# Down projection of the second token pair as seven block products, with gate and up operands stored once and read back

## The chip, the cores and the metric

The kernel runs on one core of one Trainium2 chip. The metric is the device time of one execution in microseconds (us); lower is better. The profile of a kernel is one further execution, recorded instruction by instruction on the chip. The engines of a core go by short names here: PE (TensorE, the matrix unit), DVE (VectorE), ACT (ScalarE), POOL (GpSimd), and SP, whose queue starts most of the transfers (DMA) between DRAM and on-chip memory (SBUF). PE writes into PSUM, from which DVE and ACT read.

## The reference, cut to what matters

```
x = A_x                                        # 2048 tokens, 576 features
g = sigmoid((x * gate_w).sum(-1, keepdims=True))
a = linear_attention(x, wqkv, wo)              # 32 heads
b = (gelu(x @ w_gate) * (x @ w_up)) @ w_down   # 576 -> 4608 -> 576
return g * a + (1 - g) * b
```

Everything is float32. Each factor is held as a sum of a high and a low part (float32r), and a product is three PE passes: high by high, high by low, low by high.

## The kernel before, in words

The attention part comes first, up to about 300 us. It leaves the gated attention output, 16 tiles of 128 tokens, in DRAM (`ga_d`), and the gate factors in `gate`. The rest of the span is the feed-forward part, and that is where the change lies.

**The loop.** Tokens are taken in two "pairs" of 1024, each pair as two halves of 512. The 4608 hidden features are taken in 18 blocks of 256 (`NF2`), each as two halves of 128. The loop at L830 runs `n` from 0 to 35 (`NQD` = 36): 18 blocks for the first pair, then the same 18 for the second. One turn has a gate half, `gu_steps(0)`, and an up half, `gu_steps(1)`. Each half has seven steps, s1, s6, s2, s7, s5, s4, s3, one for each of the seven block products of a Strassen-Winograd scheme over (two token halves) x (two feature halves). A product is seven matmuls of 128x512 into one PSUM bank (L664), with a stationary operand from `W[0]` (gate) or `W[1]` (up).

**Gate half.** s1's bank is copied to the tile `p1` by ACT (L715), and s2 then adds its product into the same bank, so s2 has to wait until that copy has read it. DVE forms sums of the other banks (L720, L735, L740, L749, L764), and ACT takes the gelu into four tiles `es[0]` to `es[3]`.

**Up half.** Here DVE multiplies `es[i]` by the up results (`up`, L701). In s5 and s3 the factor is first put into `p1`, the same tile as above; so the `p1` copy of the next gate half has to wait until the last `up` has read it. `high` (ACT, L704) and `low` (DVE, L707) split each `es[i]` into the tile `hs[i]`. In an ordinary turn the splits of s3's result are put off to the next gate half (`late`, L773).

**Down projection.** `down(n - 1, t)` (L780) runs one turn late, in between the steps: eight calls, one for each 128 tokens, each of 12 matmuls of 128x288 (two feature halves x three passes x two column halves) into a pair of PSUM banks, of which there are two pairs. One DVE instruction for each call (L794) multiplies by the gate factor and adds to the accumulator `acc[t]`, which was loaded with the attention output. In turn 18 four calls stand ahead of the gate half, and after the last turn eight calls end the kernel.

**Operands.** For every turn of both pairs, SP fetches the raw weights (`w_fetch`, L605), POOL forms four sums of blocks (`w_sums`, L608), ACT writes high parts and POOL low parts into `W[m]` (`w_split`, L614). `W[0]` and `W[1]` exist once each; `W[m]` can be rewritten only after PE has finished the half that reads it. `wd` is split by ACT and DVE (`d_prep`, L653). Between turns 2 and 13 POOL also forms sums of the second pair's tokens (`sums_ahead`, L669): on even turns SP fetches a piece (L674) and POOL adds. In turn 17 `renew` reloads the token operands for the second pair. Only the operands of turn 0 (`wp_d`) were made earlier, stored in DRAM and read back on the ACT queue (L627, L807).

**Order.** Everything is written out by hand: each engine executes its instructions in the order in which the code issues them, and waits on semaphores.

## Time and profile before

| What | us |
|---|---|
| Median of three timed runs | 1574.14 |
| Lowest and highest of them | 1573.69 and 1574.91 |
| The profiled execution | 1574.42 |
| Its span in the profile | 1572.7 |

| Engine | busy us | share of the span |
|---|---|---|
| PE matmul | 1556.8 | 99% |
| PE weight load | 1383.3 | 88% |
| DVE | 903.0 | 57% |
| POOL | 849.7 | 54% |
| ACT | 584.1 | 37% |

The span is the time from the first to the last recorded instruction; some 1.7 us of the profiled execution lie outside it. A row of a timeline gives start, duration, engine, source line, operation, output and inputs, and in brackets the idle time just before it and what ended it. PE's matmuls overlap at their ends, so the distance between two starts is what a group costs, and not its duration. The granted PE clock is at full speed throughout.

### The profile page before, as it was taken

The page shows a single profiled execution, that of the slowest core. Times are in us where ns is not written, and L with a number is a line of the kernel's source. Part 1 is how long each engine was busy: PE and PEld are TensorE (multiplying, and loading weights), DVE is VectorE, ACT ScalarE, POOL GpSimd, SP SyncE. Part 2 cuts the span into 40 slices and gives each one's busy share as a digit, 9 for nine tenths or more (in the row PEclk, how much of TensorE's full clock was granted, in tenths as well). Part 3 has the DMA queues.
Part 4 walks back from the last instruction along what each step waited for, and adds up shares of the span by engine and source line. Part 5 has one row for each costly group of instructions (what it writes and reads, how often), then busy time and mean ns, then how long its engine had stood idle before and what let it go on. Part 6 is the DMA issues. An engine that isn't in the chain of part 4 may idle for free.

```text
span 1572.7 us, 21574 instructions
## 1 busy us (share of the span) xinstructions
PE 1556.8 (99%) x8651; PEld 1383.3 (88%) x8651; DVE 903.0 (57%) x1265; ACT 584.1 (37%) x848; POOL 849.7 (54%) x677
## 2 busy tenths in 40 slices
PE   8999999999999999999999999999999999999998
PEld 8999788888888888888888888888888888888887
DVE  6443766465555555655555556565555555566555
ACT  6544555334333333343333323334333333333331
POOL 1400112366777777667765648655665566555650
PEclk9999999999999999999999999999999999999999
DMA  5611435712322222212211185111221121111201
GB/s 201 196 50 38 154 116 182 258 55 76 111 70 96 83 89 82 69 69 84 90 56 56 55 313 172 56 56 55 75 72 56 56 65 67 55 56 62 80 21 61
DMA packets 47964, 146.04 MB, mean 93 GB/s; under 512 B 3824, under 2 KB 20872, under 8 KB 45944
## 3 DMA queue, kind: packets, MB, share of 16 engines
q1 hardware_dynamic: 43544, 128.02, 23.9%
q10 hardware_dynamic: 2592, 9.31, 1.6%
q0 software_dynamic: 1728, 7.34, 1.2%
q8 instruction: 68, 1.11, 0.3%
q14 instruction: 32, 0.26, 0.1%
HBM read 121.16 MB, written 23.49 MB: 92 GB/s over the span
## 4 chain that ended last, share of the span: by engine, by line
PE 93%; DVE 3%; issue 1%; ACT 1%; DMA 1%; POOL 1%; SPq 0%; ACTq 0%; POOLq 0%; DVEq 0%
PE bank L664 50%; PE pair L788 29%; PE bank L169 7%; PE bank L333 3%; PE pair L524 2%; PE pair L220 1%; DMA xc<-xs 1%; POOL xo L476 1%; DVE e L701 1%; DVE h L707 0%; PE den L428 0%; PE pair L169 0%; DMA raw<-wkv 0%; PE pair L406 0%; DVE r L511 0%
## 5 line engine op out<-in xcount | busy, mean ns | idle before, releaser
L788 PEld LDWEIGHTS pair<-wd,h 128*128 128x128 f32 x3456 | 490.9, 189 | 26.4 <-DVE acc L794 3.1
L788 PE MATMUL pair<-wd,h 128*128 128x288 f32 x3456 | 505.1, 295 | 3.1 <-DVE acc L794 2.6
L664 PE MATMUL bank<-xo,wu 128*128 128x512 f32 x1764 | 434.2, 392 | 0.6 <-DVE p L740 0.5
L664 PE MATMUL bank<-xo,wg 128*128 128x512 f32 x1764 | 429.8, 392 | 1.2 <-ACT p L715 1.2
L794 DVE SCALAR_TENSOR_TENSOR acc<-pair,gate,acc 128x576 f32<-128x576 f32 x288 | 234.8, 816 | 267.9 <-PE pair L788 267.9
L664 PEld LDWEIGHTS bank<-xo,wg 128*128 128x128 f32 x1764 | 325.9, 188 | 66.7 <-ACT p L715 2.0
L664 PEld LDWEIGHTS bank<-xo,wu 128*128 128x128 f32 x1764 | 322.2, 188 | 60.9 <-DVE p L740 1.5
L704 ACT ACTIVATE h<-e 128x512 fp32r<-128x512 f32 x144 | 90.8, 630 | 403.5 <-DVE e L701 395.4
L618 POOL TENSOR_TENSOR wu<-wuraw,wu 128x768 fp32r<-128x768 f32 x35 | 70.0, 1999 | 277.4 <-ACT wu L617 277.4
L710 ACT ACTIVATE e<-e 128x512 f32<-128x512 f32 x108 | 68.3, 632 | 299.7 <-DVE e L740 118.0
L707 DVE TENSOR_TENSOR h<-e,h 128x512 fp32r<-128x512 f32 x144 | 124.8, 868 | 47.3 <-ACT h L704 47.1
L618 POOL TENSOR_TENSOR wg<-wgraw,wg 128x768 fp32r<-128x768 f32 x35 | 64.8, 1851 | 124.5 <-ACT wg L617 124.5
L169 PE MATMUL bank<-kvw,xo 128*128 128x378 f32 (+5 forms) x560 | 107.0, 345 | 5.8 <-ACT kvw L67 5.5
L169 PEld LDWEIGHTS bank<-kvw,xo 128*128 128x128 f32 (+1 forms) x560 | 97.1, 192 | 10.3 <-ACT kvw L67 6.0
L612 POOL TENSOR_TENSOR tsum<-wgraw 128x384 f32<-128x384 f32 x70 | 70.8, 1012 | 32.0 <-DMA wgraw<-wgu 29.4
L715 ACT ACTIVATE p<-bank 128x512 f32<-128x512 f32 x72 | 43.1, 598 | 119.6 <-PE bank L664 73.4
L618 POOL TENSOR_TENSOR wg<-tsum,wg 128x1024 fp32r<-128x1024 f32 x35 | 84.8, 2421 | 2.7
L618 POOL TENSOR_TENSOR wu<-tsum,wu 128x1024 fp32r<-128x1024 f32 x35 | 84.0, 2400 | 2.7
L612 POOL TENSOR_TENSOR tsum<-wuraw 128x384 f32<-128x384 f32 x70 | 83.5, 1193 | 2.7
L720 DVE TENSOR_TENSOR u<-bank,p 128x512 f32<-128x512 f32 x72 | 49.5, 688 | 41.7 <-PE bank L664 36.6
L524 PEld LDWEIGHTS pair<-kw,p 126*128 126x128 f32 (+1 forms) x480 | 65.0, 188 | 3.1 <-ACT p L512 1.2
L524 PE MATMUL pair<-kw,p 126*128 126x288 f32 (+1 forms) x480 | 66.7, 296 | 0.5 <-ACT p L512 0.3
(135 smaller groups left out, 1593.2 us busy)
## 6 DMA issues: line engine op xcount, KB each, us to landing
wgraw<-wgu SPq DMA_DIRECT2D x35, 768.0 KB, 4.2
wuraw<-wgu SPq DMA_DIRECT2D x35, 768.0 KB, 4.4
draw<-wdn SPq DMA_DIRECT2D x36, 576.0 KB, 3.7
xo<-xop_d SPq DMA_DIRECT2D x7, 1280.0 KB, 12.3
rb<-rden_d SPq DMA_DIRECT2D x8, 630.0 KB
...
```

The source lines that it names most:

```text
L169: nc.tensor.matmul(out_t[:, :n], xa, kvw[i][:rows, r, lo:lo + n], start=(k == 0), stop=(k == 13))
L333: nc.tensor.matmul(ps[:R], qw[i][:rows, rw, GO[g]:GO[g] + R], xa, start=(k == 0), stop=(k == 13))
L524: nc.tensor.matmul(y[:, i, :288], p[:R, a, g], KW[g][:R, wl, i * 288:(i + 1) * 288], start=(n == 0), stop=(n == 14))
L612: nc.gpsimd.tensor_tensor(o, a, b, OP.subtract)
L618: nc.gpsimd.tensor_tensor(w[:, i, 3:5], src[:, :, 0:2], f32(w[:, i, 0:2]), OP.subtract)
L664: nc.tensor.matmul(ps, w_, x_, start=start and i == 0, stop=i == 6, skip_group_check=not start)
L704: nc.scalar.activation(hs[i][:, 0], es[i], AF.Copy)
L707: nc.vector.tensor_tensor(hs[i][:, 1], es[i], f32(hs[i][:, 0]), OP.subtract)
L710: nc.scalar.activation(es[i], es[i], AF.Gelu_apprx_tanh)
L720: nc.vector.tensor_tensor(u2, b, p1, OP.add)
L788: nc.tensor.matmul(y[:, i, :288], h[:, a, c], wd[:, f, wl, i * 288:(i + 1) * 288], start=(k == 0), stop=(k == 5))
L794: nc.vector.scalar_tensor_tensor(a, y[:, :, :288], gate[:, 1, st:st + 1], a, op0=OP.mult, op1=OP.add)
```

## The change

1. **First pair: operands kept.** `wp_d` becomes a table with one pair of DRAM tiles for each of the 18 blocks. After each `w_split` of turns 1 to 17, SP stores `W[m]` there (2240 KB each). In the second pair no weights are fetched, summed or split from turn 19 on; instead SP loads `W[m]` whole (`w_load`).
2. **Second pair: down projection by seven products.** For turns 18 to 34 (`BLOCKS`) the eight `down` calls become 14 `unit` calls, two for each of seven block products. A unit is two groups of three matmuls of 128x288, so 84 matmuls for a turn in place of 96. Each unit ends in one DVE addition into one of seven accumulators (`sums`), without the gate factor. The operands need sums: four sums of `w_down` blocks (`d_sums`, POOL) with a split by ACT and POOL (`d_split`), and four sums of the hidden blocks (`h_sums`, POOL) with four splits (`h_parts`, ACT and POOL); the other three splits stay on ACT and DVE.
3. **Order.** `d_sums` is issued behind s2 of the up half, `d_split` behind s5, `h_sums` behind s4, and the `h_parts` behind the first three steps of the next gate half. Units stand behind the last five steps of a gate half and the first four of an up half. `acc` is not loaded for the second pair.
4. **End.** In turn 35 all 14 units stand in the gate half, three behind a step, with `combine` instructions of 128x1152 on DVE and POOL that turn seven sums into four blocks; block 35 is added by ordinary `down` calls. The gate factor and the attention output (`mix_load`) come in by eight `gated` instructions on DVE.
5. **Memory.** The first pair's tiles are freed in turn 18 and the second pair's take their place; `zmk` and some tiles move.

```
+    def w_store(n, m):
+        nc.sync.dma_start(wp_d[n % NF2][m], f32(W[m]))
+    def w_load(n, m):
+        nc.sync.dma_start(f32(W[m]), wp_d[n % NF2][m])
...
+    def d_sums():
+        b12, b11, b21, b22 = (draw[:, i] for i in range(4))
+        t1, t2, t3, t4 = (dsum[:, i] for i in range(4))
+        for o, a, b in ((t1, b12, b11), (t2, b22, t1), (t3, b22, b12), (t4, t2, b21)):
+            nc.gpsimd.tensor_tensor(o, a, b, OP.subtract)
+    def d_split():
+        for i, src in ((slice(0, 3), draw[:, 1:4]), (slice(3, 7), dsum)):
+            nc.scalar.activation(wd[:, i, 0], src, AF.Copy)
+            nc.gpsimd.tensor_tensor(wd[:, i, 1], src, f32(wd[:, i, 0]), OP.subtract)
...
+        def h_sums():
+            h_sum(es[3], es[2], es[3], OP.add)
+            h_sum(sx, es[3], es[0], OP.subtract)
+            h_sum(es[2], es[0], es[2], OP.subtract)
+            def then(i):
+                if i == 0:
+                    h_parts(S2, sx)
+                elif i == 1:
+                    h_parts(S3, es[2])
+                    h_parts(S1, es[3])
+                elif i == 2:
+                    h_sum(es[1], es[1], sx, OP.subtract)
+                    h_parts(S4, es[1])
+            return then
...
                 up(2, u3)
                 high(3)
                 low(3)
+                if blocks:
+                    late[1] = h_sums()
...
+                elif blocks:
+                    late[0] = lambda i: i == 0 and (high(1), low(1))
...
+    UNITS = [(k, q) for k in (1, 6, 4, 7, 5, 2, 3) for q in range(2)]
+    def unit(n, k, q):
+        a, b = PRODUCTS[k]
+        h, y = hb[a], pair()
+        for j in range(2):
+            c = slice((2 * q + j) * 128, (2 * q + j + 1) * 128)
+            for i, (hl, wl) in enumerate(((0, 0), (0, 1), (1, 0))):
+                nc.tensor.matmul(y[:, j, :288], h[:, hl, c], wd[:, b, wl], start=(i == 0), stop=(i == 2))
+        o = sums[:, PLACE[k], 2 * q:2 * q + 2]
+        if n == BLOCKS[0]:
+            nc.vector.tensor_copy(o, y[:, :, :288])
+        else:
+            nc.vector.tensor_tensor(o, y[:, :, :288], o, OP.add)
...
+    COMBINE = {3: [(V, 6, 6, 1, OP.add)], 4: [(V, 7, 7, 6, OP.add), (V, 4, 7, 4, OP.subtract)],
+               5: [(V, 7, 7, 5, OP.add)],
+               6: [(V, 2, 1, 2, OP.add), (G, 3, 5, 3, OP.add), (G, 3, 3, 6, OP.add)]}
...
+    def gated(t):
+        o, st = acc_of(NF2, t), PER + t
+        nc.vector.scalar_tensor_tensor(o, o, gate[:, 1, st:st + 1],
+                                       mix_of(t).rearrange("p (n c) -> p n c", n=2), op0=OP.mult, op1=OP.add)
...
         if n == NQD:
-            next_down(8)
+            next_down(2)
+            for t in range(4):
+                gated(t)
+                next_down()
+            next_down(2)
             break
...
+                if 0 < n < NF2:
+                    w_store(n, 1)
+                if n > NF2:
+                    w_load(n, 1)
                 if 2 <= n < 14:
                     sums_ahead(n // 2 - 1, n % 2)
+            if i == 3 and n > NF2:
+                d_fetch(n)
+            if n - 1 in BLOCKS:
+                if i >= 2:
+                    next_down(3 if last else 2)
+                if last:
+                    combine(*COMBINE.get(i, []))
+            elif i >= 3:
                 next_down()
...
-        for i, step in enumerate(gu_steps(1, final)):
+        for i, step in enumerate(gu_steps(1, final, blocks)):
             step()
-            if i == 0 and n + 1 < NQD:
+            if i == 0 and n < NF2:
                 w_split(0)
-                if n + 2 < NQD:
+                if n + 1 < NF2:
                     w_fetch(n + 2, 0)
+                    w_store(n + 1, 0)
                 w_sums(1)
+            if i == 0 and second and not last:
+                w_load(n + 1, 0)
+            if blocks and i == 2:
+                d_sums()
             if i < 4:
                 next_down()
-            if i == 3:
-                if final:
-                    d_prep()
-                    if n + 1 < NQD:
-                        d_fetch(n + 1)
+            if i == 3 and final:
+                d_prep()
+            if blocks and i == 4:
+                d_split()
             if turn_over:
                 renew(i)
+            if last and i in (2, 3):
+                gated(2 * i)
+                gated(2 * i + 1)
```

More of the change, by code (lines that the diff above doesn't have):

```diff
@@ L48, in tile_gated_mix @@
     gate = keep.tile([128, 2, NST], F32, name="gate")
-    zmk = keep.tile([128, NG, 128], F32R, name="zmk")
     rden_d = {(b, h): dram.tile([7 * NG, BS // 2], F32, name=f"rden_d{b}{h}") for b in range(NB) for h in range(2)}
@@ L52, in tile_gated_mix @@
     ga_d = [dram.tile([128, D], F32, name=f"ga_d{i}") for i in range(NST)]
-    wp_d = [dram.tile([128, 7, 5, 128], F32, name=f"wp_d{m}") for m in range(2)]
+    wp_d = [[dram.tile([128, 7, 5, 128], F32, name=f"wp_d{n}_{m}") for m in range(2)] for n in range(NF2)]
     def f32(ap):
@@ L284, in store @@
         def store(self):
-            nc.sync.dma_start(wp_d[self.m][:, :, self.kt], f32(self.hi))
+            nc.sync.dma_start(wp_d[0][self.m][:, :, self.kt], f32(self.hi))
             if self.kt < 2:
-                nc.sync.dma_start(wp_d[self.m][:, :, 3 + self.kt], f32(self.lo))
+                nc.sync.dma_start(wp_d[0][self.m][:, :, 3 + self.kt], f32(self.lo))
     early = []
@@ L323, in tile_gated_mix @@
     KW = [kwp.tile([128, 2, D], F32R, name=f"kw{g}") for g in range(NG)]
+    zmk = kwp.tile([128, NG, 128], F32R, name="zmk")
     r_of = {}
@@ L626, in tile_gated_mix @@
     scaled(0, 0)
-    nc.scalar.dma_start(f32(W[0]), wp_d[0])
+    nc.scalar.dma_start(f32(W[0]), wp_d[0][0])
     mixed(3, 3)
@@ L648, in tile_gated_mix @@
     NQD = NP * NF2
+    BLOCKS = range(NF2, NQD - 1)
     def d_fetch(n):
@@ L653, in d_prep @@
     def d_prep():
-        split(wd[:, :, 0], wd[:, :, 1], draw)
+        split(wd[:, :4, 0], wd[:, :4, 1], draw)
+    def d_sums():
[7 more added lines that the diff above has]
+            nc.gpsimd.tensor_tensor(wd[:, i, 1], src, f32(wd[:, i, 0]), OP.subtract)
     def product(k, m, ps, start):
@@ L665, in product @@
                              skip_group_check=not start)
-    ahead, late = {}, []
+    ahead, late = {}, {}
     def sums_ahead(k, part):
@@ L693, in renew, with gu_steps @@
         nc.sync.dma_start(f32(xo[:, a]), xop_d[:, a])
-    def gu_steps(m, seam=False):
+    def gu_steps(m, seam=False, blocks=False):
         ps = {}
@@ L707, in low, with h_sum, h_parts @@
             nc.vector.tensor_tensor(hs[i][:, 1], es[i], f32(hs[i][:, 0]), OP.subtract)
+        def h_sum(o, a, b, op):
+            nc.gpsimd.tensor_tensor(o, a, b, op)
+        def h_parts(a, src):
+            nc.scalar.activation(hb[a][:, 0], src, AF.Copy)
+            nc.gpsimd.tensor_tensor(hb[a][:, 1], src, f32(hb[a][:, 0]), OP.subtract)
+        def h_sums():
[12 more added lines that the diff above has]
+            return then
         def gelu(i):
@@ L755, in s4 @@
                 low(3)
+                if blocks:
+                    late[1] = h_sums()
         def s3():
             d = ps["d"]
-            if m == 1:
+            if m == 1 and not blocks:
                 high(2)
@@ L771, in s3 @@
                     low(1)
+                elif blocks:
+                    late[0] = lambda i: i == 0 and (high(1), low(1))
                 else:
-                    late.append(lambda: (high(1), low(2), low(1)))
+                    late[0] = lambda i: i == 0 and (high(1), low(2), low(1))
         return [s1, s6, s2, s7, s5, s4, s3]
@@ L778, in acc_load, with acc_of @@
         nc.sync.dma_start(acc[t], ga_d[p * PER + t])
+    def acc_of(n, t):
+        if n < NF2:
+            return acc[t].rearrange("p (n c) -> p n c", n=2)
+        return sums[:, 0:2, t] if t < 4 else sums[:, 2:7:4, t - 4]
     def down(n, t):
@@ L787, in down @@
                 for i in range(2):
-                    nc.tensor.matmul(y[:, i, :288], h[:, a, c], wd[:, f, wl, i * 288:(i + 1) * 288],
+                    nc.tensor.matmul(y[:, i, :288], h[:, a, c], wd[:, (1 - i, 2 + i)[f], wl],
                                      start=(k == 0), stop=(k == 5))
                 k += 1
-        a = acc[t].rearrange("p (n c) -> p n c", n=2)
+        a = acc_of(n, t)
         p, q = divmod(n, NF2)
@@ L795, in down, with place, combine, mix_of @@
         if q == NF2 - 1:
-            nc.sync.dma_start(out[st * 128:(st + 1) * 128, :], acc[t])
-            if p + 1 < NP:
-                acc_load(p + 1, t)
+            nc.sync.dma_start(out[st * 128:(st + 1) * 128, :].rearrange("p (n c) -> p n c", n=2), a)
+    PLACE = {2: 0, 3: 1, 4: 2, 5: 3, 1: 4, 6: 5, 7: 6}
+    UNITS = [(k, q) for k in (1, 6, 4, 7, 5, 2, 3) for q in range(2)]
[11 more added lines that the diff above has]
+            nc.vector.tensor_tensor(o, y[:, :, :288], o, OP.add)
+    def place(k):
+        return sums[:, PLACE[k]].rearrange("p j c -> p (j c)")
+    def combine(*parts):
+        for eng, o, a, b, op in parts:
+            eng.tensor_tensor(place(o), place(a), place(b), op)
+    V, G = nc.vector, nc.gpsimd
+    COMBINE = {3: [(V, 6, 6, 1, OP.add)], 4: [(V, 7, 7, 6, OP.add), (V, 4, 7, 4, OP.subtract)],
+               5: [(V, 7, 7, 5, OP.add)],
+               6: [(V, 2, 1, 2, OP.add), (G, 3, 5, 3, OP.add), (G, 3, 3, 6, OP.add)]}
+    def mix_of(t):
+        v = dsum.rearrange("p b c -> p (b c)") if t in (4, 5) else place({3: 1, 0: 5, 1: 6}[t // 2])
+        return v[:, t % 2 * D:(t % 2 + 1) * D]
+    def mix_load(t):
+        nc.sync.dma_start(mix_of(t), ga_d[PER + t])
+    def gated(t):
+        o, st = acc_of(NF2, t), PER + t
+        nc.vector.scalar_tensor_tensor(o, o, gate[:, 1, st:st + 1],
+                                       mix_of(t).rearrange("p (n c) -> p n c", n=2), op0=OP.mult, op1=OP.add)
     first_steps = gu_steps(0)
@@ L806, in tile_gated_mix @@
     scaled(1, 0)
-    nc.scalar.dma_start(f32(W[1]), wp_d[1])
+    nc.scalar.dma_start(f32(W[1]), wp_d[0][1])
     first_steps[3]()
@@ L815, in tile_gated_mix @@
     mlp.banks(4)
-    mp = mlp.pool("mp")
+    hp0 = mlp.pool("hp0")
+    es += [hp0.tile([128, BS], F32, name=f"e{i}") for i in range(1, 4)]
+    hs = [hp0.tile([128, 2, BS], F32R, name=f"h{i}") for i in range(4)]
+    one = Scope()
+    mp = one.pool("mp")
     wraw += [mp.tile([128, 4, 3, 128], F32, name=n) for n in ("wgraw", "wuraw")]
@@ L819, in tile_gated_mix @@
     w_fetch(1, 0)
-    acc = [mp.tile([128, D], F32, name=f"acc{i}") for i in range(NST // NP)]
-    wd = mp.tile([128, 2, 2, D], F32R, name="wd")
-    draw = mp.tile([128, 2, D], F32, name="draw")
-    es += [mp.tile([128, BS], F32, name=f"e{i}") for i in range(1, 4)]
-    hs = [mp.tile([128, 2, BS], F32R, name=f"h{i}") for i in range(4)]
-    xup = mlp.pool("xup")
+    acc = [mp.tile([128, D], F32, name=f"acc{i}") for i in range(PER)]
+    wd = mp.tile([128, 4, 2, 288], F32R, name="wd")
+    draw = mp.tile([128, 4, 288], F32, name="draw")
+    xup = one.pool("xup")
     for t in range(PER):
@@ L830, in tile_gated_mix @@
     for n in range(NQD + 1):
-        seam = n % NF2 == 0
-        order_ = [4, 5, 6, 7, 0, 1, 2, 3] if seam else range(8)
-        downs = deque((lambda t=t: down(n - 1, t)) for t in order_) if n else deque()
+        seam, last = n % NF2 == 0, n == NQD - 1
+        second = n >= NF2
+        blocks = n in BLOCKS
+        if n - 1 in BLOCKS:
+            downs = deque((lambda u=u: unit(n - 1, *u)) for u in UNITS)
+        elif n:
+            downs = deque((lambda t=t: down(n - 1, t)) for t in ([4, 5, 6, 7, 0, 1, 2, 3] if seam else range(8)))
+        else:
+            downs = deque()
         def next_down(k=1):
@@ L845, in tile_gated_mix @@
         final = (n + 1) % NF2 == 0
-        turn_over = final and n + 1 < NQD
+        turn_over = final and not last
         for i, step in enumerate(gu_steps(0) if n else first_steps):
@@ L849, in tile_gated_mix @@
                 step()
-            if i == 0 and late:
-                late.pop()()
+            for k in sorted(late):
+                late[k](i)
             if i == (0 if n else EARLY - 1):
-                if n and not seam:
+                if n and not second:
                     d_prep()
                     d_fetch(n)
-                if n:
+                if 0 < n <= NF2:
                     w_split(1)
-                if n + 1 < NQD:
+                if n < NF2:
                     w_fetch(n + 1, 1)
@@ L860, in tile_gated_mix @@
                     w_sums(0)
+                if 0 < n < NF2:
+                    w_store(n, 1)
+                if n > NF2:
+                    w_load(n, 1)
                 if 2 <= n < 14:
                     sums_ahead(n // 2 - 1, n % 2)
-            if i >= 3:
-                next_down()
-        for i, step in enumerate(gu_steps(1, final)):
+            if i == 3 and n > NF2:
+                d_fetch(n)
+            if n - 1 in BLOCKS:
+                if i >= 2:
[3 more added lines that the diff above has]
+            elif i >= 3:
+                next_down()
@@ new lines, in tile_gated_mix @@
+        late.clear()
+        if n == NF2:
+            one.close()
+            two = Scope()
+            mp = two.pool("mp2")
+            sums = mp.tile([128, 7, 4, 288], F32, name="sums")
+            wd = mp.tile([128, 7, 2, 288], F32R, name="wdb")
+            draw, dsum = (mp.tile([128, 4, 288], F32, name=x) for x in ("draw2", "dsum"))
+            sx = mp.tile([128, BS], F32, name="sx")
+            hx = [mp.tile([128, 2, BS], F32R, name=f"hx{i}") for i in range(3)]
+            hb = {A11: hs[0], A12: hs[1], A22: hs[3], S3: hs[2], S1: hx[0], S2: hx[1], S4: hx[2]}
+            d_fetch(n)
@@ L866, in tile_gated_mix @@
+        if last:
+            for t in (4, 5, 6, 7, 0, 1, 2, 3):
+                mix_load(t)
+        for i, step in enumerate(gu_steps(1, final, blocks)):
             step()
-            if i == 0 and n + 1 < NQD:
+            if i == 0 and n < NF2:
                 w_split(0)
-                if n + 2 < NQD:
+                if n + 1 < NF2:
                     w_fetch(n + 2, 0)
+                    w_store(n + 1, 0)
                 w_sums(1)
+            if i == 0 and second and not last:
+                w_load(n + 1, 0)
+            if blocks and i == 2:
+                d_sums()
@@ L872, in tile_gated_mix @@
             if i < 4:
                 next_down()
-            if i == 3:
-                if final:
-                    d_prep()
-                    if n + 1 < NQD:
-                        d_fetch(n + 1)
+            if i == 3 and final:
+                d_prep()
+            if blocks and i == 4:
+                d_split()
             if turn_over:
                 renew(i)
+            if last and i in (2, 3):
+                gated(2 * i)
+                gated(2 * i + 1)
+    two.close()
@@ L917 @@
     wgu = np.stack([blocks(wg), blocks(wu)], axis=1)
-    wdn = wd.reshape(NF2, 2, 128, D).transpose(0, 2, 1, 3)
+    h = wd.reshape(NF2, 2, 128, 2, D // 2)
+    wdn = np.stack([h[:, 0, :, 1], h[:, 0, :, 0], h[:, 1, :, 0], h[:, 1, :, 1]]).transpose(1, 2, 0, 3)
     cst = np.zeros((128, CW), np.float32)
```

## The prediction

> **What bounds the kernel now.** I read the page first, then the chain that ended last in order of time, then the timelines of PE, DVE, POOL and ACT around an up half and the gate half behind it, since a wait there would be hidden in the page's averages.

> ```profile
> span 1572.7 us, 21574 instructions
> PE 1556.8 (99%) x8651; PEld 1383.3 (88%) x8651; DVE 903.0 (57%) x1265; ACT 584.1 (37%) x848; POOL 849.7 (54%) x677
> PE 93%; DVE 3%; issue 1%; ACT 1%; DMA 1%; POOL 1%; SPq 0%; ACTq 0%; POOLq 0%; DVEq 0%
> ```

> The chain, in order of time:

> ```profile
> 1477.97 11.29 PE bank L664 x49
> 1513.25 11.29 PE bank L664 x49
> 1558.71 9.86 PE pair L788 x72
> ```

> And PE's timeline in turn 35, from the start of its gate half:

> ```profile
> 1517.92 6.62 PE L664 MATMUL bank<-xo,wg 128*128 128x512 f32 x28
> 1524.37 1.76 PE L788 MATMUL pair<-wd,h 128*128 128x288 f32 x12
> 1525.96 0.40 PE L664 MATMUL bank<-xo,wg 128*128 128x512 f32 x1
> ```

> PE sets the end. A turn takes 1513.25 - 1477.97 = 35.28 us. Four products take 1524.37 - 1517.92 = 6.45 us, so 1.61 us each, and a `down` of 12 matmuls takes 1.59 us: 14 x 1.61 + 8 x 1.59 = 35.3 us, the whole turn. PE has no idle time in an ordinary turn. So matmuls taken away count in full, as long as nothing new makes PE wait. Two mechanisms of this kernel decide that.

> **First mechanism: the tile `p1`.** Here are an ordinary up half's end (PE, DVE, ACT) and the one turn boundary where it goes wrong (turn 18 to 19), in the same order:

> ```profile
> 349.99 6.62 PE L664 MATMUL bank<-xo,wg 128*128 128x512 f32 x28
> ...
> 351.22 0.69 DVE L701 TENSOR_TENSOR e<-p,e 128x512 f32<-128x512 f32 x1
> ...
> 352.01 0.60 ACT L715 ACTIVATE p<-bank 128x512 f32<-128x512 f32 x1 [1.30 <-DVE e L701]
> ```

> ```profile
> 956.55 3.50 PE L664 MATMUL bank<-xo,wg 128*128 128x512 f32 x14 [0.58 <-ACT p L715]
> ...
> 955.02 0.79 DVE L701 TENSOR_TENSOR e<-p,e 128x512 f32<-128x512 f32 x1
> ...
> 955.90 0.60 ACT L715 ACTIVATE p<-bank 128x512 f32<-128x512 f32 x1 [2.28 <-DVE e L701]
> ```

> I put zero at a turn's first gate product (349.99 in the first fence). The last `up` ends at 1.92, the ACT copy starts 0.10 later and takes 0.60, and s2 may start 0.05 after that: at 2.67. PE reaches s2 only at 2 x 1.61 = 3.22. The margin is 0.55 us. In the second fence it is gone, and PE stands still. So s2 starts at (end of the last `up`) + 0.75, and every delay of that `up` beyond 0.55 us is paid on PE.

> **Second mechanism: DVE and POOL get in each other's way.** DVE and POOL around the `low` at 377.23 of turn 2, then those of turn 18's up half:

> ```profile
> 376.72 1.29 POOL L619 TENSOR_TENSOR wg<-tsum,wg 32x512 fp32r<-32x512 f32 x1
> 378.09 1.34 POOL L612 TENSOR_TENSOR tsum<-wuraw 128x384 f32<-128x384 f32 x1
> ...
> 377.23 1.33 DVE L707 TENSOR_TENSOR h<-e,h 128x512 fp32r<-128x512 f32 x1 [0.70 <-ACT h L704]
> ```

> ```profile
> 947.73 0.69 DVE L707 TENSOR_TENSOR h<-e,h 128x512 fp32r<-128x512 f32 x1 [0.70 <-ACT h L704]
> 948.34 0.68 DVE L735 TENSOR_TENSOR u<-bank,u 128x512 f32<-128x512 f32 x1
> 950.29 0.95 DVE L701 TENSOR_TENSOR e<-p,e 128x512 f32<-128x512 f32 x1
> ...
> 947.90 2.79 POOL L618 TENSOR_TENSOR wg<-tsum,wg 128x1024 fp32r<-128x1024 f32 x1
> ```

> A DVE instruction with both inputs in SBUF (`up`, `low`) that meets a running POOL sum ends 0.55 us after it: POOL ends at 378.01, `low` at 378.56; POOL at 950.69, `up` at 951.24. A POOL sum that meets such a DVE instruction ends its own time less 0.15 us after it: 378.56 + 1.02 - 0.15 = 379.43; 948.42 + 2.42 - 0.15 = 950.69 (its undisturbed times are below). The instruction at 948.34, with one input from PSUM, runs at full speed inside the POOL sum. They take turns, and I use the same rule for the long sums of the change.

> [...]

> **Prices** (page, costliest groups, and the groups kept apart by shape):

> ```profile
> L618 POOL TENSOR_TENSOR wg<-tsum,wg 128x1024 fp32r<-128x1024 f32 x35 | 84.8, 2421 | 2.7
> L618 POOL TENSOR_TENSOR wg<-wgraw,wg 128x768 fp32r<-128x768 f32 x35 | 64.8, 1851 | 124.5 <-ACT wg L617 124.5
> L612 POOL TENSOR_TENSOR tsum<-wgraw,tsum 128x384 f32<-128x384 f32 x35 | 35.5, 1015 | 2.7
> L67 ACT ACTIVATE wd<-draw 128x1152 fp32r<-128x1152 f32 x36 | 41.7, 1158 | 7.0 <-PE pair L788 7.0
> L704 ACT ACTIVATE h<-e 128x512 fp32r<-128x512 f32 x144 | 90.8, 630 | 403.5 <-DVE e L701 395.4 <-PE bank L664 8.1
> L68 DVE TENSOR_TENSOR wd<-draw,wd 128x1152 fp32r<-128x1152 f32 x36 | 49.3, 1370 | 12.5 <-ACT wd L67 12.5
> L720 DVE TENSOR_TENSOR u<-bank,p 128x512 f32<-128x512 f32 x72 | 49.5, 688 | 41.7 <-PE bank L664 36.6 <-ACT wg L617 2.6 <-ACT wu L617 2.5
> L794 DVE SCALAR_TENSOR_TENSOR acc<-pair,gate,acc 128x576 f32<-128x576 f32 x288 | 234.8, 816 | 267.9 <-PE pair L788 267.9
> ```

> By interpolation, as estimates from these rows: POOL 128x864 (three blocks of `d_split`) 2.05 us, 128x1152 (four blocks) 2.67, 128x512 (`h_sums`) 1.29; ACT 128x864 0.92; a DVE addition of a unit between 0.69 and 0.82, I take 0.77.

> **Gain.** Turns 19 to 35 do 84 matmuls in place of 96, in the same form: half a `down`, 0.795 us, for a unit. An undisturbed turn takes 14 x 1.61 + 14 x 0.795 = 33.7 us, 1.59 less. Over 17 turns that is 27.0 us. DVE gets 14 x 0.77 in place of 8 x 0.82, still under PE. POOL loses the weight sums, but its new work falls elsewhere in the turn.

> **Loss in an ordinary turn.** Through a turn boundary, zero at the first gate product: the last unit leaves PE at -3 x 1.61 = -4.84. PE's end reaches ACT 0.25 later, as it did where a split waited for the last `down` of turn 16, first PE's next group, then ACT:

> ```profile
> 909.63 3.38 PE L664 MATMUL bank<-xo,wu 128*128 128x512 f32 x14
> ...
> 909.88 1.17 ACT L67 ACTIVATE wd<-draw 128x1152 fp32r<-128x1152 f32 x1 [3.48 <-PE pair L788]
> ```

> ACT's copy of three blocks runs to -3.67, and POOL's `lo1` from -3.59 to -1.54. On DVE, s5's `p1` ends at -2.33; its `up` meets `lo1` and ends at -0.98. `lo2` (1152) was queued behind it and ends at -0.98 + 2.67 - 0.15 = 1.54. The `up` of s4 arrives at -0.32, in the middle of `lo2`, and ends at 2.09. `low` follows to 2.70. The first `h_sum` rewrites `es[3]`, so it waits for that `low`, and runs from 2.78 to 4.07. s3's `p1` on DVE ends at 3.30; the last `up` arrives at 3.33, meets the `h_sum`, and ends at 4.62 in place of 1.92. So s2 starts at 5.37 in place of 3.22: a stall of 2.15 us against a gain of 1.59. Each ordinary turn becomes 35.83 us, 0.55 longer than before. Over turns 20 to 34 that is 15 x 0.55 = +8.2. The next possible wait, S2's low part for unit 6, is ready at about 8.9 and PE reaches it only at 10.2: nothing is added.

> **Turn 19.** `d_fetch` of turn 18 goes out only when the first pair's tiles are free, near the start of the up half, so `d_sums` ends about 9.3 us after that start and the chain above runs later by some 1.4 us: a stall of 3.5 us there. Before, this boundary had its own stall of 0.58 in the trace, 0.74 by the rule. Net 3.5 - 0.74 - 1.59 = +1.2.

> **End.** In turn 35 three units follow each other over two PSUM pairs, so every third waits for a DVE addition, with five `combine` instructions of 1.37 us (row L68) in the same queue: the gate half takes 27.7 us for an undisturbed 22.4, 2.15 of the difference by `p1`. Two POOL `combine` instructions of 2.67 us then hold up DVE, which still has `d_prep`, four `gated` and the splits in its queue: s3 of the up half waits 4.5 us until DVE has read its bank, and the last eight `down` calls lose 1.8. From the turn's start to PE's end I get 58.0 us. Before it was 1568.57 - 1517.92 = 50.65, with stalls of its own. Net +7.4, the saving of the turn's units included.

> **First pair.** Stores and loads, by the transfers of the same size and kind (core's timelines, windows of 2 us; the last columns are DMA share and GB/s):

> ```profile
> 280.12 0.33 ACTq L807 DMA_DIRECT2D wu<-wp_d  x1
> ...
> 358.77 0.63 SPq L674 DMA_DIRECT2D xu<-xs  x1
> ...
> 366.30 0.74 POOL L458 TENSOR_TENSOR xu<-xu 128x256 f32<-128x256 f32 x1
> ```

> ```profile
> 178.00:180.00 2.00, 2.00 (x13) 1.74 (x11) 1.29 (x1) 0.60 (x1) 0.74 (x1) 1.00 1.01 420
> ...
> 284.00:286.00 2.00, 2.00 (x17) 2.00 (x16) 1.56 (x2) 0.30 (x1) 0.00 (x0) 1.00 1.02 439
> 286.00:288.00 2.00, 2.00 (x17) 2.00 (x16) 0.09 (x1) 1.48 (x2) 0.00 (x0) 1.00 0.80 335
> 288.00:290.00 2.00, 2.00 (x17) 2.00 (x16) 1.48 (x2) 0.03 (x1) 0.00 (x0) 1.00 0.25 90
> ```

> A load of `W[m]` issued at 280.12 is over by 290, under 10 us. The shortest window between the last use of `W[0]` and its next is an up half of 7 x 1.61 + 4 x 0.795 = 14.5 us: hidden, and if it were not, each us too late would cost 16. A store of 2.29 MB at 420 GB/s takes 5.5 us. On SP's queue `w_store` waits for POOL's whole split, and on turns 2, 4 to 12 the fetch of `xu` stands behind it: issued at about 362.6 and not 358.77, landing at about 371.5 behind the store. POOL, which was ready for it at 366.30, waits, and its following sums end 3 to 5 us later, where they meet the `up` and `low` of s5 to s3. By the same two rules the last `up` slips by 0.9 us, 0.35 beyond the margin. Bounds: 0 if the store is quicker, 1 us a turn if not. I take 6 x 0.35 = +2. Everything else in the first pair keeps its place: 18 turns without a difference.

> **Sum.** +2 (first pair) + 1.2 (turn 19) + 8.2 (turns 20 to 34) + 7.4 (end) = +18.8. The profiled execution took 1574.42 (0.28 above the median of the runs, which is nothing here): 1593.2 us.

> **Rivals.** *The collisions are off the path (faster).* PE stays the bound in turns 19 to 34: 16 x 1.59 = 25.4 gained and the old 0.74 too, the end costs +4 since only PSUM pairs and DVE's queue count there: 1574.4 - 26.1 + 4 = 1552 us. For it: DVE and POOL are little over half busy, and no ordinary turn of before shows a stall. Against it: all of POOL's new work that needs the last unit or the last `up` is issued into the same 9 us in which DVE has its five instructions with two SBUF inputs. It decides at a stall of 1.59 us: below that each ordinary turn wins. *The last `up` gets ahead of the `h_sum`.* Then it ends at 4.0 and the stall is 1.5: turns even out, 1574.4 + 2 + 0.6 - 0.8 + 7 = 1583 us, still slower. Against it: the `h_sum` is ready half a us earlier. *Loads of W become the bound:* each gate half would wait for `W[0]`; with 4.5 us of room I give it next to nothing.

> **How the numbers follow.** My forecast, with its own range of 1583 to 1603 (stall 1.5 to 2.6 us a turn, first pair 0 to 6, end 4 to 9), has 0.62; the second rival 0.08; the first rival, whole or in part (a stall under about 1 us), 0.24; in between, 0.06. A measurement of this kernel can tell about 0.2%, 3 us, from no change. That makes faster 0.24, same 0.06, slower 0.70. The range from 1560 to 1603 leaves out the lower part of the first rival and little above.

> **What would show it.** Right: PE's timeline has a gap of about 2 us at s2 of every gate half from turn 20 on, ended by ACT's `p1` (L715 of before); the `up` behind s4 lasts over 2 us; the distance of turns is 35.8 us; PE's busy share falls while its matmuls fall by 204. Wrong: turns of 33.7 us with no gap; or a gap ended by `W`, by `hx` (S2's split) or by a PSUM pair; or a first pair whose turns are not 35.28 us on odd turns.

## The result and the profile after

The changed kernel takes 1627.05 us (median of six runs, 1622.14 to 1628.18); the kernel before takes 1574.12 (six runs, 1573.69 to 1574.91). The ratio is 1.0329, with a 95% interval of 1.0315 to 1.0343: slower, as forecast, but by 52.9 us where 18.8 were forecast, and beyond the upper end of the range, 1603. The profiled execution took 1624.2 us, its span 1622.4, 49.7 more than before.

From the page of the changed kernel: the span, the share of the engines in the chain that ended last, and the group of the gate products, with its idle time and what ended it behind the second bar.

```profile
span 1622.4 us, 21214 instructions
PE 1564.7 (96%) x8447; PEld 1378.1 (85%) x8447; DVE 1009.5 (62%) x1346; ACT 547.1 (34%) x848; POOL 820.0 (51%) x645
PE 83%; DVE 11%; ACT 2%; issue 1%; DMA 1%; POOL 1%; SPq 0%; ACTq 0%; POOLq 0%; DVEq 0%
...
L684 PE MATMUL bank<-xo,wg 128*128 128x512 f32 x1764 | 445.8, 398 | 38.5 <-ACT p L759 38.0
```

PE has the 204 matmuls less that were foreseen, and yet it is busy 1564.7 us and not 1556.8. So the matmuls that are left took longer. Beside that, 38.0 us of idle time stand ahead of gate products, all ended by ACT's copy to `p1` (L759, the L715 of before).

**Where the 49.7 us lie.** Starts of gate halves on PE's timeline cut the span:

| Stretch | before | after | difference | forecast |
|---|---|---|---|---|
| to the first gate product of the loop | 297.73 | 298.19 | +0.5 | 0 |
| from there to turn 18 | 625.93 | 632.90 | +7.0 | +2 |
| turns 18 and 19 | 65.06 | 67.61 | +2.5 | +1.2 |
| turns 20 to 34 | 529.2 | 559.98 | +30.8 | +8.2 |
| turn 35 to the end of the span | 54.8 | 63.7 | +8.9 | +7.4 |

Most of what was missed, 22.6 of 30.9 us, lies in the ordinary turns. Two of them and the start of a third on PE's timeline (start, duration, engine, line, operation):

```profile
1186.38 3.38 PE L684 MATMUL bank<-xo,wg 128*128 128x512 f32 x14
1191.70 1.89 PE L684 MATMUL bank<-xo,wg 128*128 128x512 f32 x7 [1.94 <-ACT p L759]
...
1222.38 3.38 PE L684 MATMUL bank<-xo,wg 128*128 128x512 f32 x14
1227.71 1.89 PE L684 MATMUL bank<-xo,wg 128*128 128x512 f32 x7 [1.94 <-ACT p L759]
...
1258.39 1.78 PE L684 MATMUL bank<-xo,wg 128*128 128x512 f32 x7
```

s2 starts 1191.70 - 1186.38 = 5.32 us after the first gate product; 5.37 was forecast. The turns take 36.00 and 36.01 us; 35.83 was forecast. But only these two turns of the 15 look like this. The other 13 take 37.52 to 37.57, say 37.54 us, and here is one of them:

```profile
1111.32 3.39 PE L684 MATMUL bank<-xo,wg 128*128 128x512 f32 x14
1116.64 2.09 PE L684 MATMUL bank<-xo,wg 128*128 128x512 f32 x7 [1.94 <-ACT p L759]
1118.53 3.08 PE L862 MATMUL pair<-wdb,h 128*128 128x288 f32 x12
1121.41 1.87 PE L684 MATMUL bank<-xo,wg 128*128 128x512 f32 x7
```

The gap is the same, 1.94 us, and s2 again starts at 5.32. But the 12 unit matmuls behind it cost 1121.41 - 1118.53 = 2.88 us, where 12 such matmuls cost 1.61 in the turns above. Stretches of half a microsecond of this turn give the reason (PE busy with its count, granted clock, DMA share, GB/s):

```profile
1116.00:1116.50 0.50, 0.00 (x0) 1.00 0.83 358
1117.50:1118.00 0.50, 0.50 (x4) 1.00 0.92 394
1118.00:1118.50 0.50, 0.50 (x3) 0.66 0.75 323
1118.50:1119.00 0.50, 0.50 (x3) 0.50 0.82 338
...
1121.00:1121.50 0.50, 0.50 (x4) 0.50 0.00 0
1121.50:1122.00 0.50, 0.50 (x4) 0.93 0.00 0
```

A mean of 0.66 is a third of the stretch at full clock, so the granted clock falls to half at about 1118.2, 1.5 us behind the end of the gap; by the 0.93 it comes back at about 1121.6. Over stretches of 40 us (PE, PEld, DVE, ACT, POOL, clock, DMA share, GB/s) the one from 1180 to 1220, which lies for the most part in a quick turn, shows a full clock:

```profile
1140.00:1180.00 40.00, 38.06 (x197) 33.23 (x196) 26.60 (x34) 10.36 (x16) 19.13 (x14) 0.96 0.35 132
1180.00:1220.00 40.00, 38.06 (x203) 32.98 (x203) 28.80 (x36) 11.71 (x17) 20.40 (x15) 1.00 0.34 130
```

PE is busy 38.06 us in both, but with 197 matmuls in one and 203 in the other: busy time alone hides this loss. By an estimate half a clock for 3.4 us costs at most 0.5 x 3.4 = 1.7 us; measured it is 37.54 - 36.00 = 1.53 a turn.

DVE, POOL and ACT at the same boundary, in this order, one fence each:

```profile
1109.02 1.28 DVE L721 TENSOR_TENSOR e<-p,e 128x512 f32<-128x512 f32 x1
...
1110.94 2.46 DVE L721 TENSOR_TENSOR e<-u,e 128x512 f32<-128x512 f32 x1
...
1114.64 1.26 DVE L721 TENSOR_TENSOR e<-p,e 128x512 f32<-128x512 f32 x1
```

```profile
1109.72 3.13 POOL L674 TENSOR_TENSOR wdb<-dsum,wdb 128x1152 fp32r<-128x1152 f32 x1
1114.08 1.27 POOL L731 TENSOR_TENSOR e<-e,e 128x512 f32<-128x512 f32 x1 [1.23 <-DVE h L727]
```

```profile
1115.99 0.60 ACT L759 ACTIVATE p<-bank 128x512 f32<-128x512 f32 x1 [5.02 <-DVE e L721]
```

The chain is the forecast one, link by link. The first `up` ends at 1110.30; `lo2` meets it and ends at 1112.85 (1110.30 + 2.67 - 0.15 = 1112.82). The `up` of s4 meets `lo2` and ends at 1113.40, which is 1112.85 + 0.55. The last `up` meets the first `h_sum`, which ends at 1115.35, and ends itself at 1115.90, 0.55 later and 4.58 after the first gate product (forecast 4.62). Then comes ACT's copy, and then s2. The `up` of s4 waited 2.46 - 0.69 = 1.77 us. In the whole trace of the kernel before no `up` or `low` lasted over 1.51 us, which is a wait of 0.82.

### The profile page after: what moved, and what is told of

Same layout as the page of the kernel before. It is cut to its first block, busy times and chain, and to the rows that moved or that the text cites. A ratio compares the mean times of both kernels' runs of the same rounds, so it can differ in the third digit from the quotient of the medians.

```text
span 1622.4 us, 21214 instructions
## 1 busy us (share of the span) xinstructions
PE 1564.7 (96%) x8447; PEld 1378.1 (85%) x8447; DVE 1009.5 (62%) x1346; ACT 547.1 (34%) x848; POOL 820.0 (51%) x645
## 4 chain that ended last, share of the span: by engine, by line
PE 83%; DVE 11%; ACT 2%; issue 1%; DMA 1%; POOL 1%; SPq 0%; ACTq 0%; POOLq 0%; DVEq 0%
PE bank L684 42%; PE pair L841 15%; PE pair L862 13%; PE bank L168 7%; DVE e L721 6%; PE bank L333 3%; PE pair L524 2%; PE pair L219 1%; DVE h L727 1%; ACT p L759 1%; DVE p L784 1%; DVE p L810 1%; DVE u L793 1%; DMA xc<-xs 1%; POOL xo L476 1%
## 5 line engine op out<-in xcount | busy, mean ns | idle before, releaser
L841 PEld LDWEIGHTS pair<-wd,h 128*128 128x128 f32 x1728 | 245.2, 189 | 14.6 <-DVE acc L847 1.6
L841 PE MATMUL pair<-wd,h 128*128 128x288 f32 x1728 | 252.0, 294 | 1.6 <-DVE acc L847 1.3
L867 DVE TENSOR_TENSOR sums<-pair,sums 128x576 f32<-128x576 f32 x224 | 169.2, 757 | 55.1 <-PE pair L862 47.3
L847 DVE SCALAR_TENSOR_TENSOR acc<-pair,gate,acc 128x576 f32<-128x576 f32 x144 | 117.4, 816 | 133.7 <-PE pair L841 133.7
L674 POOL TENSOR_TENSOR wdb<-draw,wdb 128x864 fp32r<-128x864 f32 x17 | 35.5, 2086 | 256.1 <-ACT wdb L673 256.1
L862 PEld LDWEIGHTS pair<-wdb,h 128*128 128x128 f32 x816 | 137.5, 219 | 10.6 <-DVE sums L867 2.1
L862 PE MATMUL pair<-wdb,h 128*128 128x288 f32 x816 | 141.2, 326 | 1.6 <-DVE sums L867 1.6
L759 ACT ACTIVATE p<-bank 128x512 f32<-128x512 f32 x72 | 43.1, 599 | 185.7 <-DVE e L721 102.5
L618 POOL TENSOR_TENSOR wu<-wuraw,wu 128x768 fp32r<-128x768 f32 x18 | 36.0, 1999 | 129.2 <-ACT wu L617 129.2
L862 PEld LDWEIGHTS pair<-wdb,hx 128*128 128x128 f32 x612 | 89.2, 189 | 6.1 <-ACT e L754 0.5
L862 PE MATMUL pair<-wdb,hx 128*128 128x288 f32 x612 | 93.0, 296 | 0.2 <-DVE sums L867 0.2
L721 DVE TENSOR_TENSOR e<-p,e 128x512 f32<-128x512 f32 x72 | 75.5, 1049 | 2.5
```

The costliest lines, as they stand in the source:

```text
L721: nc.vector.tensor_tensor(es[i], v, es[i], OP.mult)
L759: nc.scalar.activation(p1, ps["a"], AF.Copy)
L841: nc.tensor.matmul(y[:, i, :288], h[:, a, c], wd[:, (1 - i, 2 + i)[f], wl], start=(k == 0), stop=(k == 5))
L847: nc.vector.scalar_tensor_tensor(a, y[:, :, :288], gate[:, 1, st:st + 1], a, op0=OP.mult, op1=OP.add)
L862: nc.tensor.matmul(y[:, j, :288], h[:, hl, c], wd[:, b, wl], start=(i == 0), stop=(i == 2))
L867: nc.vector.tensor_tensor(o, y[:, :, :288], o, OP.add)
```

## Experiments

The open question is what the 30.8 us of the ordinary turns are made of. The theory: the stall at `p1` comes from DVE and POOL taking turns, and the half clock follows from the gap that the stall leaves, so both go if the gap goes. Against it stand: the loads of `W`, 2240 KB each, which run at the same time, bring the clock down; or PE waits for something of the new units as well.

**1. s3 of the up half no longer uses `p1`.** It puts its factor into `u3`, a tile of the up half that is free by then. The wait stays, but nothing of the next gate half hangs on it.

```
-            nc.vector.tensor_tensor(es[1] if m == 0 else p1, d, u2, OP.add)
+            nc.vector.tensor_tensor(es[1] if m == 0 else u3, d, u2, OP.add)
...
-                up(1, p1)
+                up(1, u3)
```

> The changed kernel, with s3's sum of the up half in the tile u3 in place of p1, so that the copy of p1 in the next gate half no longer waits for the last up. Loads, units and POOL's work stay. Theory A (the wait for p1 makes the gap at s2, and the gap makes the half clock behind it): no gap at s2, granted clock 1.00 in all ordinary turns, a small wait of up to 0.5 us at unit 6 for S2's low part, turns of 33.9 to 34.4 us in place of 37.5 and 36.0; odd turns of the first pair back at 35.3; total 1560 to 1572 us. Theory B (the half clock follows the loads of W, 2240 KB at over 400 GB/s, which run just then): the gap goes but the clock still falls to 0.5 for 3.4 us a turn, turns near 35.7, total near 1590. Theory C (another wait stands right behind p1, on the bank that u2 frees or on DVE's queue): the gap moves and turns stay over 35.5.

Measured: 1569.85 us (six runs, 1568.78 to 1571.08) beside 1575.01 for the kernel before on the same chip; ratio 0.9967, interval 0.9954 to 0.9979. That is 57 us less than the changed kernel, by one tile. PE's timeline has no gap at s2 any more, the 21 matmuls of s1, s6 and s2 follow each other, and one small wait of 0.27 us shows at the second pair of units, for their operand `hx` (S2's split):

```profile
1171.56 1.60 PE L862 MATMUL pair<-wdb,hx 128*128 128x288 f32 x10 [0.27 <-POOL hx L735]
...
1197.13 5.00 PE L684 MATMUL bank<-xo,wg 128*128 128x512 f32 x21
1201.97 1.77 PE L862 MATMUL pair<-wdb,h 128*128 128x288 f32 x12
```

Stretches of 40 us (PE alone, clock, DMA share, GB/s):

```profile
1140.00:1180.00 40.00, 39.73 (x218) 1.00 0.35 130
1180.00:1220.00 40.00, 39.74 (x216) 1.00 0.43 160
```

Turns 20 to 34 take 34.3 to 34.4 us, and the clock is full while the same loads of `W` move the same bytes. So in this run the loads did not lower it: it was 1.00 at 130 and at 160 GB/s. The first pair lost its slips as well: its odd turns take 35.33, because there, too, `p1` was what PE waited for. The end still waits 3.67 us at s3.

**2. The fetch of `xu` ahead of the store of `W[1]`.** Of the first pair alone.

```
-                if 0 < n < NF2:
-                    w_store(n, 1)
...
                     sums_ahead(n // 2 - 1, n % 2)
+                if 0 < n < NF2:
+                    w_store(n, 1)
```

> The changed kernel, with the store of W[1] issued behind the fetch of xu on SP's queue, nothing else. Theory A: odd turns 3 to 13 lose their gap of 0.69 at s2 and the turns of the first pair are 35.3 throughout, 6.2 us less in all, nothing changes behind turn 18. Rival (the stores slow the first pair by themselves, by traffic): the odd turns stay at 36.3.

One run: 1621.08 us. Turn 18 starts at 924.95 and not at 931.09, 6.1 us earlier, and the odd turns of the first pair take 35.33. So the order on SP's queue is what cost the first pair its time, by way of the wait for `p1` that experiment 1 takes away as well. The second pair stays as it was, with 14 of the 15 ordinary turns at 37.53 to 37.56 and one at 36.01; only turn 19 came out longer, 39.39, with a gap of 3.74 us.

**3. POOL's low parts in seven pieces.** `d_split` gives POOL seven instructions of 288 columns in place of 864 and 1152, so that DVE can get in between.

```
-            nc.gpsimd.tensor_tensor(wd[:, i, 1], src, f32(wd[:, i, 0]), OP.subtract)
+            for j in range(i.stop - i.start):
+                k = i.start + j
+                nc.gpsimd.tensor_tensor(wd[:, k, 1], src[:, j], f32(wd[:, k, 0]), OP.subtract)
```

> The changed kernel, with POOL's two low parts of w_down (864 and 1152 columns) written as seven instructions of 288, same data and same order. Theory A with turn-taking (DVE waits for one POOL instruction at most): the up behind s4 lasts about 1.3 and not 2.46 us, the last up ends at about 3.1 behind the first gate product and not 4.6, the gap at s2 is 0.4 to 0.7 us, no half clock, turns of 34.3 to 34.7, total near 1578. Rival (it is the amount of POOL's work that delays DVE, or POOL goes ahead of DVE each time): the gap stays at 1.7 or more, and turns at 36 to 37.5.

One run: 1588.42 us. PE's timeline:

```profile
1172.92 3.38 PE L686 MATMUL bank<-xo,wg 128*128 128x512 f32 x14
1177.36 1.89 PE L686 MATMUL bank<-xo,wg 128*128 128x512 f32 x7 [1.06 <-ACT p L761]
...
1208.06 2.25 PE L686 MATMUL bank<-xo,wg 128*128 128x512 f32 x9
```

The gap shrinks to 1.06 us, more than the expected size, and the turn to 1208.06 - 1172.92 = 35.14. The clock is full in all 15 turns (0.999 on the mean of the run). So the length of POOL's instructions makes the larger part of the wait, as the rule of taking turns has it, but the sum for short pieces came out too low. DVE's timeline shows why. The `up` of s4 lasts 1.19 us, but the `low` and the last `up` behind it meet a piece each as well:

```profile
1173.34 1.30 DVE L729 TENSOR_TENSOR h<-e,h 128x512 fp32r<-128x512 f32 x1
...
1175.27 1.35 DVE L723 TENSOR_TENSOR e<-p,e 128x512 f32<-128x512 f32 x1
```

That `low` took 0.68 us in the changed kernel. The 0.62 more are what the expectation was short of: the last `up` ends at 1176.62, 3.70 us behind the first gate product and not 3.1.

**4. A gap made by hand in the kernel before.** Extra ACT copies into `p1` stand ahead of the real one: three in turns 20 to 23, four in 24 to 27, five in 28 to 31, six in 32 to 35. This kernel has neither loads of `W` nor units.

```
+            for _ in range(extra):
+                nc.scalar.activation(p1, es[1], AF.Copy)
...
+        for i, step in enumerate(gu_steps(0, extra=n // 4 - 2 if n >= 20 else 0) if n else first_steps):
```

> The kernel before, with ACT kept busy ahead of the p1 copy from turn 20 on, by copies of 128x512 into p1 that are written over: 3 copies in turns 20 to 23, 4 in 24 to 27, 5 in 28 to 31, 6 in 32 to 35. No loads of W, no units, POOL's work as before. Gaps at s2 of about 1.0, 1.5, 2.0 and 2.5 us. Theory A: turns longer by the gap (about 36.3, 36.8, 37.3, 37.9), and from some gap at or below 2 us on also the half clock for 3.4 us, 1.5 us more; for 3 copies none. Theory B (loads of W): the clock stays at 1.00 whatever the gap.

One run: 1623.84 us. The starts of the gate halves give:

| Gap on PE | lengths of the turns | with the half clock |
|---|---|---|
| 1.22 | 36.78, 36.77, 36.78, 36.78 | 0 of 4 |
| 1.88 | 39.01, 37.43, 37.43, 37.44 | 1 of 4 |
| 2.54 | 38.09, 39.67, 39.36, 39.67 | 3 of 4 |
| 3.20 | 38.75, 40.31, 40.32 | 2 of 3 |

(The last turn, 35, has no next one to measure it by.)

PE's timeline, at the first two turns with the gap of 1.88:

```profile
1136.26 3.38 PE L664 MATMUL bank<-xo,wg 128*128 128x512 f32 x14
1141.52 5.08 PE L664 MATMUL bank<-xo,wg 128*128 128x512 f32 x14 [1.88 <-ACT p L717]
```

```profile
1175.27 3.38 PE L664 MATMUL bank<-xo,wg 128*128 128x512 f32 x14
1180.54 3.50 PE L664 MATMUL bank<-xo,wg 128*128 128x512 f32 x14 [1.89 <-ACT p L717]
```

After the same gap, the same 14 matmuls last 5.08 us in the one and 3.50 in the other. The clock records of the trace show what differs. The six falls behind these gaps begin at 1141.99, 1333.14, 1370.68, 1411.64, 1490.15 and 1531.11 us, and the steps from one to the next are 56, 11, 12, 23 and 12 times 3.413 us. With the time cut into windows of 3.413 us that end at these points, the gap of the slow turn lies in the first window below, and that of the quick turn in the second and third (PE busy with its count, granted clock, DMA share, GB/s):

```profile
1138.58:1141.99 3.41, 1.53 (x7) 1.00 0.00 0
1176.13:1179.54 3.41, 2.52 (x11) 1.00 0.00 0
1179.54:1182.95 3.41, 2.42 (x10) 1.00 0.00 0
```

The first gap lies whole in one window, and the clock falls at that window's end; the second is split between two, and it doesn't fall. So here a gap alone brought the half clock, with no transfer running beside it (a DMA share of 0.00), and whether it did went with its place in these windows and not with its length alone (more under the last heading). Without it the gap cost its delay: a gap shown as 1.88 made the turn 37.43 - 35.28 = 2.15 us longer.

**5. The gaps taken away, and S2's split first.** Edits 1 and 2, and in `h_sums` the third sum put behind S2's split, so that POOL reaches `hx` sooner.

```
             h_sum(sx, es[3], es[0], OP.subtract)
-            h_sum(es[2], es[0], es[2], OP.subtract)
...
                     h_parts(S2, sx)
+                    h_sum(es[2], es[0], es[2], OP.subtract)
```

> The kernel with s3's sum in u3, with two further edits: the store of W[1] behind the fetch of xu, and S2's split ahead of the third sum of hidden blocks on POOL, so that unit 6 finds S2's low part about 1 us earlier. Theory A: the wait of 0.27 us at unit 6 for POOL goes, each ordinary turn falls from 34.34 to 33.9 us (15 x 0.45 = 6.6 us in all), total near 1563. If the third sum, now later, becomes the next wait (unit 7), turns stay above 34.2.

Measured: 1559.52 us (four runs, 1559.09 to 1561.40) beside 1574.52; ratio 0.9902, interval 0.9885 to 0.9918. PE's timeline has no wait left in an ordinary turn:

```profile
1194.21 5.00 PE L684 MATMUL bank<-xo,wg 128*128 128x512 f32 x21
1199.06 1.77 PE L862 MATMUL pair<-wdb,h 128*128 128x288 f32 x12
1200.66 1.79 PE L684 MATMUL bank<-xo,wg 128*128 128x512 f32 x7
1202.28 1.75 PE L862 MATMUL pair<-wdb,hx 128*128 128x288 f32 x12
```

Turns 20 to 34 take 33.80 us, where the prediction had 33.7 for an undisturbed one. They gain 15 x 1.48 = 22.2 us on the kernel before. The end, 61.2 us for 54.8, gives back 6.4.

**6. The end as well.** Edit 5; in turn 35 one `combine` and the low part of `d_prep` go from DVE to POOL, and `gated` 6 and 7 behind s3.

```
-    COMBINE = {3: [(V, 6, 6, 1, OP.add)], 4: [(V, 7, 7, 6, OP.add), (V, 4, 7, 4, OP.subtract)],
+    COMBINE = {3: [(V, 6, 6, 1, OP.add)], 4: [(V, 7, 7, 6, OP.add), (G, 4, 7, 4, OP.subtract)],
...
+        eng = nc.gpsimd if last else nc.vector
+        eng.tensor_tensor(wd[:, :4, 1], draw, f32(wd[:, :4, 0]), OP.subtract)
...
-            if last and i in (2, 3):
-                gated(2 * i)
-                gated(2 * i + 1)
+            if last and i in (2, 6):
+                gated(i // 2 + 3 if i == 2 else 6)
+                gated(i // 2 + 4 if i == 2 else 7)
```

> As the one with S2 first, and in turn 35 three edits: one of the two combine instructions behind s5 and the low part of block 35's w_down on POOL and not on DVE, and the gated instructions for tiles 6 and 7 behind s3 and not s7. If DVE's queue sets the end: s3 of the last up half no longer waits 3.67 us, the half clock behind it goes too (1.7 us), the wait of 1.56 us at the units shrinks; 5 to 7 us less than without these edits, total near 1557. If POOL's 1152-column instructions are then in the way of DVE: 0 to 3 us less.

Measured: 1559.46 us (four runs, 1558.29 to 1559.78), ratio 0.9901, interval 0.9886 to 0.9916: no different from 5. The wait in the gate half fell from 1.56 to 0.15 us, but s3 still waits, and the last `down` calls now wait 1.92 us for DVE, where they waited 0.36 in 5. POOL and DVE of this kernel:

```profile
1522.83 6.48 POOL L877 TENSOR_TENSOR sums<-sums 128x1152 f32<-128x1152 f32 x2 [3.74 <-DVE sums L869]
1529.32 3.05 POOL L665 TENSOR_TENSOR wdb<-draw,wdb 128x1152 fp32r<-128x1152 f32 x1
```

```profile
1529.78 3.94 DVE L893 SCALAR_TENSOR_TENSOR sums<-sums,gate,dsum 128x576 f32<-128x576 f32 x2
...
1534.43 0.69 DVE L786 TENSOR_TENSOR p<-bank,u 128x512 f32<-128x512 f32 x1
```

The two `gated` on DVE, both inputs in SBUF, take 3.94 us, where two of them took 1.53 in the changed kernel (at 1595.59), because POOL's low part runs from 1529.32 to 1532.37. The `p1` factor behind them frees s3's bank only then, and PE waits 3.55 us for it. Work moved from DVE to POOL came back as waiting on DVE.

**7. The stored operands alone, in the kernel before.** The store and the load of `W`, with the down projection as it was.

```
+                if 0 < n < NF2:
+                    w_store(n, 1)
+                if n > NF2:
+                    w_load(n, 1)
...
+                    w_store(n + 1, 0)
...
+            if i == 0 and n >= NF2 and n + 1 < NQD:
+                w_load(n + 1, 0)
```

> The kernel before, with only the first half of the change: weights stored by the first pair and loaded by the second; the down projection is that of before. Theory A: PE stays the bound; turns of the second pair 35.28 as before or a little more if a transfer were late, the odd turns 3 to 13 of the first pair 1.0 us longer as in the changed kernel; total 1580. If the loads slow PE or its clock: second-pair turns over 35.5.

One run: 1596.27 us, about 16 more than expected. The odd turns 3 to 13 take 36.24 to 36.33 us, 6 us in all, and the ordinary turns of the second pair 35.28, as before, at full clock (1.00 in each stretch of 40 us from 980 to 1540): those loads are hidden. What was not expected is one wait, at the first load:

```profile
973.12 8.89 PE L670 MATMUL bank<-xo,wg 128*128 128x512 f32 x28 [13.85 <-DMA wg<-wp_d]
```

Here the load for turn 19 stands on SP's queue behind the `out` and `acc` transfers of turn 18's last `down` calls, and behind this wait the clock is at half again for a time (28 gate matmuls in 8.73 us for 6.45, and a mean of 0.83 from 940 to 980). The changed kernel doesn't load `acc` for the second pair, and there the same wait is 0.45 us. So this run shows what the loads cost in ordinary turns, which is nothing, but its total is not the share of the change.

**8. Without POOL's low part of `w_down`** in the block turns but the first.

```
-    def d_split():
+    def d_split(low):
...
-            nc.gpsimd.tensor_tensor(wd[:, i, 1], src, f32(wd[:, i, 0]), OP.subtract)
+            if low:
+                nc.gpsimd.tensor_tensor(wd[:, i, 1], src, f32(wd[:, i, 0]), OP.subtract)
```

> The changed kernel, leaving out POOL's low part of w_down in all block turns but the first (the low parts of the first are used again). Theory A: the up behind s4 takes 0.7 us and not 2.46, the last up still meets the first sum of hidden blocks and ends at about 2.5, the gap at s2 is 0.1 us or none, no half clock, turns 33.9 to 34.2, total 1570 to 1576 with the first pair and the end as in the changed kernel. Rival (the sums of hidden blocks alone are enough to delay the last up): gap over 0.8 us.

One run: 1570.02 us. Ordinary turns take 33.95 us with no gap at s2; the 21 matmuls of s1, s6 and s2 follow each other:

```profile
1168.38 5.15 PE L685 MATMUL bank<-xo,wg 128*128 128x512 f32 x21
```

At the one boundary where the low part still stands, turn 19, the gap is 3.55 us and the turn 39.24. So without these two POOL instructions there is no stall in an ordinary turn. The last `up` still meets the first `h_sum`, which is still there, and ends 2.52 us behind the first gate product, where 2.47 costs PE nothing. What the two would do without the `h_sum` was not tried.

## Why the prediction was wrong

The sign and the mechanism were right, and so was the stall; the price of the stall was not.

- *"Loss in an ordinary turn"* is the step that failed. It put a stall of 2.15 us against a gain of 1.59 and took 0.55 x 15 = 8.2 us. The stall came out as 5.32 - 3.22 = 2.10 us (experiments 1 and 8 show that it is `p1` and POOL's low parts that make it). But the sum took the matmuls behind the stall at their price of before. In 13 of 15 turns PE's clock was at half for some 3.4 us behind the gap: 13 x 1.53 = 19.9 us that no term held. The rest of the 30.8 is 15 x 0.72 = 10.8, a turn at full clock (36.00 for 35.28): 8.2 plus 0.17 a turn, of which 0.10 is the undisturbed turn (33.80 and not 33.7); the rest is not split further. The wait of the `up` of s4 behind `lo2` in that sum, 2.09 + 0.32 - 0.69 = 1.72 us, was an estimate that no row of the kernel before showed; the run showed 1.77.
- *First pair.* The mechanism was right, the size not: +7.0 for +2. POOL waited for `xu` as foreseen:

```profile
443.67 0.74 POOL L458 TENSOR_TENSOR xu<-xu 128x256 f32<-128x256 f32 x1 [5.09 <-DMA xu<-xs]
```

  That is the upper end of the 3 to 5 us, and PE's gap behind it, at 461.62, is 0.69 us. An odd turn loses 36.34 - 35.28 = 1.06, six of them 6.4; I took 0.35 and named 1 as the upper bound. Experiment 2 gives 6.1 back. Odd turns other than 35.28 were also named as a sign of being wrong, which did not agree with the 0.35 that the sum itself put there.
- *Turn 19.* +2.5 for +1.2: a wait of 0.45 for the first load of `W[0]`, and a gap of 2.19 at s2, less than the 3.5 of the sum, with the half clock behind it (0.50 from 968.2 to 971.2). Over the runs that keep `p1` this gap varied from 0.88 (experiment 3) to 3.74 (experiment 2).
- *End.* +8.9 for +7.4. PE's timeline of the changed kernel:

```profile
1583.45 1.07 PE L862 MATMUL pair<-wdb,h 128*128 128x288 f32 x6 [1.56 <-DVE sums L867]
...
1587.59 9.83 PE L684 MATMUL bank<-xo,wu 128*128 128x512 f32 x42
1601.10 3.35 PE L684 MATMUL bank<-xo,wu 128*128 128x512 f32 x7 [3.68 <-DVE p L784]
```

  The gate half took 1587.59 - 1558.68 = 28.91 us for 27.7, with the half clock behind its stall (0.50 from 1565.5 to 1568.5). s3 waited 3.68 us for 4.5, and its seven matmuls cost 3.15 for 1.61, at half clock once more (0.50 from 1599.6 to 1606). That the whole came so near is in part luck: the wait at s3 and the loss of the last eight calls (about 1.0 for 1.8) were put 1.6 us too high, which made up for most of the half clock that the sum did not hold.
- *The first rival* (collisions off the path, 1552 us) asked for a stall under 1.59 us, and the stall was 2.10. Experiment 5 is what it described, with the collisions still there but nothing waiting on them: 1559.5. *The last `up` gets ahead of the `h_sum`* did not happen: the `h_sum` started at 1114.08 and the `up` at 1114.64. *Loads of W as the bound* got next to nothing, rightly for ordinary turns.
- *"The one turn boundary where it goes wrong"* is a misreading that changes no sum. The kernel before has the same gap of 0.58 us at the boundary from turn 0 to turn 1 as well (317.82), and the changed kernel has it there too (0.57).

One thing stays open. Which gaps between 1.2 and 3.2 us are followed by the half clock goes, in these traces, with where they lie in the windows of 3.413 us; that is read from the traces, and no run was made to move a gap within its window and so bring the fall about or keep it away.
